# Delta-rule attention with a feed-forward block on one core: six weight tiles load later, ScalarE's unpacking copies and some Grams, D and lane copies change places

## The chip, the cores and the metric

The kernel runs on one core of one Trainium2 chip. The metric is the device time of one execution in microseconds. A core has five engines with queues of their own: TensorE (PE, its weight loads PEld), VectorE (DVE), ScalarE (ACT), GpSimd (POOL) and SyncE (SP), which here issues nearly all DMAs. Each works through its instructions in program order; semaphores order them against one another.

## What is computed

```python
# q, k, v: batch 4, 8 heads, 768 steps, head size 48; beta: one number per head and step
k_n = k / (np.linalg.norm(k, axis=-1, keepdims=True) + 1e-06)
for t in range(S):                                   # state: 48 x 48 per batch and head
    y[:, :, t] = q[:, :, t] @ state
    state = state + beta_t * outer(k_t, v_t - k_t @ state)
x = y.transpose(0, 2, 1, 3).reshape(3072, 384)
h = x @ w_in                                         # w_in: 384 x 2048
g = np.where(h >= 1, h, np.where(h <= -1, 0, (h + 1) ** 2 / 4))
out = g @ w_out                                      # w_out: 2048 x 384
```

First a linear attention with a delta rule (a recurrence over the sequence), then two matrix products with a function between them.

## The kernel before, in words

**The recurrence.** The 768 steps are cut into 12 chunks of 64 (g = 0 to 11). Two chunks make a block (G = 0 to 5, NS = 6). For one block `lanes`, `solve` (or `solve_whole` for blocks from the third on) and `unlanes` invert a small triangular system on VectorE: `gram` (L141) forms the products of the keys on TensorE; ScalarE evicts them to `GG` (L150) and, for g below 4, to `W` (L155, with a select on GpSimd), later VectorE masks them into `W` (L163). `lanes` (L190) copies them (L202, a step for each of the two chunks), transposes them (L204, a step of its own), forms the norms (L207 to L214, in the next step), and for G from 2 on also multiplies by the signs (L217) and lets GpSimd select (L218). `solve_whole` (L241) takes 30 steps of two VectorE instructions each (L247, L249), all in place, `unlanes_whole` ends it (L255, L257, L260). `merge16` and `merge32` (L277 to L329) put the parts of the inverse together on TensorE, with ScalarE's copies between (L314, L316, L328). Then each chunk goes through a chain on TensorE: `chain_r` (L334; VectorE subtracts in L343), `chain_u` (ScalarE evicts to `SU` in L356), `chain_y` (evicted in L377 and L378, rest in L381 and L382, and six DMAs on SP in L386 that complete the input `xb` of the matrix products), `chain_d` (the state's change, D; for the first chunk ScalarE evicts it in L401, for all others VectorE adds it in L407). `scale_v` (L180) scales v by the norms (L184, a step for each half). The PSUM tile `ch` has two buffers, and Grams, merges and chain pieces share it; each chain piece and each pair of Grams takes both.

**The matrix products.** They are cut into items: for a block, 16 tiles f of the 2048 columns. The first block has 24 items, since its two chunks come to hand one after the other: 8 items on the first half, 8 on both, 8 on the second half; every other block has 16. An item does `up` (L522) into PSUM tile `h`, a relu and a square on ScalarE (L644 twice, L663), a maximum on VectorE (L671), splits the result into a high part on ScalarE (`ghi`, L639) and a rest on VectorE (`glo`, L640), and two items later `down` (L537). `store` (L540) ends a block.

**The weights.** A tile f holds 128 rows of both matrices as 64-bit patterns (768 KB). `weight_loads` (L80) loads it on SP; `weight` (L120) unpacks it in six steps: ScalarE L125 into one of four buffers of `X4`, VectorE L127, L129, L131, ScalarE L135 (the high part), VectorE L137 (the rest), which frees the buffer. `unpack` (L428) deals these steps out, four portions to a tile; `run(wu, n)` hands out n portions. 26 portions (tiles 0 to 6) are given out in the stages of the prologue, the others in the items, four in each.

**The order.** It is written out by hand. Up to line 497 stands a prologue for the first block: loads, Grams, twenty matmuls of `hold` (L469), solve, merges and the chain of chunk 0, with portions of `unpack` between; then the main loop over the items (L647). `plan` (L556) puts pieces of the next block's work at slots of the current block: a slot is half an item, `pe` holds TensorE's pieces, `fill` VectorE's portions and the loads. An item runs in this order: evictions left from the slot before, `rest` of the last item (ghi, glo), `up`, the first relu, the `pe` pieces of its first slot, a portion of `unpack`, the `fill` of that slot, the pieces' evictions, a portion of `unpack`, second relu and square, `down`, the `pe` pieces of its second slot, the maximum, two portions of `unpack`, the `fill` of the second slot. In `plan`, a and b are the two chunks of the next block, T is 5 for G = 0 and 1 after that. SP issues its DMAs in program order too: after the loads of the start come the six of L386, the loads of W and KV for the chunk after next (`load_w`, `load_kv`), the stores.

Of the kernel before, what the change touches and what calls it, by code (L numbers as in the profile page):

```python
# [20 lines left out]
FT = DF // 128  # L21
WARM = 14
KEEP = 20
PASSES = ((0, 0), (0, 1), (1, 0))
WHOLE = 2
LAG = 2


@with_exitstack
def delta_rule_moe(ctx: ExitStack, tc: tile.TileContext, kqa, kqb, kv, beta, w, out):  # L30
# [14 lines left out]
    nc = tc.nc  # L45
# [13 lines left out]
    W, KV, XB, RAW, WT = {}, {}, {}, {}, {}  # L59
# [15 lines left out]
    def load_kv(g, q=nc.sync):  # L75
        for i in range(NT):
            KV[g, i] = sb.tile([P, 2, NV, D], F32, name="KV", bufs=4)
            q.dma_start(out=KV[g, i], in_=kv[g, i])

    def weight_loads(n0, n1):  # L80
        for f in range(n0, n1):
            RAW[f] = const.tile([P, 2, 2 * DM], F32, name=f"wt{f}")
            nc.sync.dma_start(out=RAW[f].bitcast(I32), in_=w.bitcast(I32)[:, f])


# [4 lines left out]
    weight_loads(0, 2)  # L90
    load_kv(0)
    load_kv(1)
    weight_loads(2, FT)

    warm = sb.tile([P, P], F32, name="wx")
    nc.vector.memset(warm, 0.0)
# [83 lines left out]
    def scale_v(g):  # L180

        for i in range(NT):
            v, u = KV[g, i][:, 1], g % 2 * NU + i * NV
            nc.vector.tensor_tensor(out=v, in0=v, in1=S["N"][:, u:u + NV, None].broadcast_to([P, NV, D]), op=ALU.mult)  # L184
            yield
# [4 lines left out]
    def lanes(G):  # L190

        A = S["A"] = sb.tile([P, 32, 32], F32, name="A", bufs=1)
        if G < WHOLE:
            X = S["X"] = sb.tile([P, 2, 16, 16], F32, name="X", bufs=1)
# [20 lines left out]
        yield  # L215
        if G >= WHOLE:
            nc.vector.scalar_tensor_tensor(out=A, in0=A, scalar=-1.0, in1=gm[:, :, None].broadcast_to([P, 32, 32]), op0=ALU.mult, op1=ALU.mult)  # L217
# [199 lines left out]
    def products(*pieces):  # L417
        return [p() for p in pieces]

    def both(f, g):  # L420
        return [lambda i=i: f(g, i) for i in range(NT)]
# [6 lines left out]
    def unpack():  # L428

        gens = [weight(f) for f in range(FT)]  # L430

        def step(f):
            if f < FT:
                next(gens[f])
        step(0)
        step(1)
        for f in range(FT + 2):
            if f < FT:
                step(f)
                yield  # L440
            if f > 1:
                step(f - 2)
                yield
            step(f + 2)
            if f < FT:
                step(f)
                yield
                step(f)
                step(f)
                yield  # L450


    def stage(pieces, *fill):
        evicts = products(*pieces)
        for gen, m in fill:
            run(gen, m)
        finish(evicts)

    spare += START
    wu, sv, ln, raws = unpack(), [scale_v(0), scale_v(1)], lanes(0), []  # L460
# [29 lines left out]
    load_w(2)  # L490
    stage(both(chain_d, 0), (wu, 1))
    load_kv(2)
    for q, r in enumerate(QS):
        for x in range(2):
            nc.gpsimd.dma_start(out=beta_sb[r + 16 * x:r + 16 * x + 16, 1:NS, :], in_=beta[q:64:4, 2 + x:ntot:2, :])
# [51 lines left out]
    pe, fill = {}, {}  # L547

    def at(where, G, t, *x):
        where.setdefault(2 * first[G] + int(round(2 * t)), []).extend(x)  # L550

    def grams(G, t, g, dt=0.5):
        for j in range(2):
            at(pe, G, t + j * dt, *[lambda i=2 * j + x: gram(g, i) for x in range(2)])

    def plan(G):  # L556

        a, b = 2 * G + 2, 2 * G + 3
        if G < NS - 1:
            ln, so, un, va, vb = lanes(G + 1), solve(), unlanes(), scale_v(a), scale_v(b)  # L560
        if G == 0:
            at(pe, G, 0, *both(chain_y, 1))
            at(fill, G, 1, (load_w, 3))
            at(pe, G, 1, *both(chain_d, 1))
            at(fill, G, 1.5, (load_kv, 3))
            grams(G, 2, a)
            grams(G, 4, b)
            at(fill, G, 4, (ln, 1))
            at(fill, G, 5, (ln, 1))
            at(fill, G, 5.5, (ln, 1))  # L570
            at(fill, G, 6, (ln, 9))
            for j in range(8):
                at(fill, G, 6.5 + j / 2, (so, 2))
            at(fill, G, 9, (va, 1))
            at(fill, G, 9.5, (va, 1))
            at(fill, G, 10.5, (un, 1))
            at(fill, G, 11, (un, 9))
            at(fill, G, 13, (vb, 1))
            at(fill, G, 14, (vb, 1))
            T = 5  # L580
        elif G < NS - 1:
            so, un = solve_whole(), unlanes_whole()
            for j in range(2):
                at(fill, G, 2 + j, (va, 1))
                at(fill, G, 11 + j, (vb, 1))
            at(fill, G, 0.5, (ln, 2))
            at(fill, G, 1, (ln, 1))
            at(fill, G, 1.5, (ln, 9))
            cost, H = 0, 0
            for j in range(1, 31):  # L590
                at(fill, G, 2.5 + H / 2, (so, 1))
                cost += j * (31 - j) + 150
                H = int(cost / 9461 * 14)
            for j in range(4):
                at(fill, G, 9.5 + j // 2 / 2, (un, 1))
            T = 1
        if G < NS - 1:
            if G == 0:
                for j, f in enumerate((merge16_a, merge16_b, merge32_a, merge32_b)):
                    for g in range(2):  # L600
                        at(pe, G, T + 7 + j + g / 2, lambda f=f, g=g: f(g))
            else:
                for j, f in enumerate((merge32_a, merge32_b)):
                    for g in range(2):
                        at(pe, G, 10.5 + j + g / 2, lambda f=f, g=g: f(g))
            at(pe, G, T + 6.5, *both(chain_r, a))
            at(pe, G, T + 11, *both(chain_u, a))
            at(pe, G, T + 11.5, *both(chain_y, a))
            at(pe, G, T + 12, *both(chain_d, a))
            at(pe, G, T + 12.5, *both(chain_r, b))  # L610
            at(pe, G, T + 13, *both(chain_u, b))
            at(pe, G, T + 13.5, *both(chain_y, b))
            if G < NS - 2:
                at(fill, G, T + 12, (load_w, a + 2))
                at(fill, G, T + 12.5, (load_kv, a + 2))
                late = 0 if G == 0 else 2
                at(pe, G, T + 14 + late, *both(chain_d, b))
                at(fill, G, T + 14, (load_w, b + 2))
                at(fill, G, T + 14.5 + late, (load_kv, b + 2))
                grams(G, T + 14 + (G == 0) / 2, a + 2)  # L620
                grams(G, T + 14.5 + (G == 0), b + 2)

    for G in range(NS):
        plan(G)
# [21 lines left out]
    late, last, ready = [], None, []  # L646
    for n, item in enumerate(items):  # L647
# [15 lines left out]
        nc.scalar.activation(out=s[:, c], in_=s[:, c], func=AF.Square)  # L663
        if len(ready) == LAG:
            x = ready.pop(0)
# [4 lines left out]
        late = products(*pe.pop(H + 1, []))  # L670
# [6 lines left out]
    G = NS - 1  # L677
# [50 lines left out]
```

## Time and profile before

| | us |
|---|---|
| median of 3 runs | 718.3 (716.6 to 722.27) |
| the profiled execution | 714.19 |
| its span, first to last instruction | 712.2 |
| TensorE busy | 646.0 |
| VectorE busy | 440.7 |
| ScalarE busy | 400.1 |
| GpSimd busy | 45.1 |

The profile is one execution. A line of a view gives a source line of the kernel, an engine, an operation and tiles (written <- read). In the chain and in the timeline the first number is the start in microseconds from the start of the span, the second the duration. In windows each engine has its busy time in the stretch and its number of instructions, then come the granted TensorE clock (1.00 is full), the DMA engines' mean busy share and GB/s. In groups, "busy, mean ns | idle before <- releaser" gives the engine's idle time just before these instructions and what ended most of it. TensorE's records count each 32-bit matmul of the program as two.

### The profile page before, as it was taken

To read this page: it belongs to the slowest core of one execution; us is meant where nothing else is said; L and a number is where in the kernel's file an instruction comes from. 1 tells how busy PE (TensorE), PEld (TensorE's weight loads), DVE (VectorE), ACT (ScalarE), POOL (GpSimd) and SP (SyncE) were. 2 spreads that over 40 slices of the span, in tenths; PEclk is the share of its full clock that TensorE was granted. 3 is DMA by queue.
4 is the path that set the end of the run, shared out by engine and by line. 5 is a ranking of instruction groups with operands and counts; after the bars stand their busy time and mean duration, and the time that the engine had idled before them with its cause. 6 is when DMAs were issued, how large, how long until landed. Compare 5 with 4: busy or idle time off the path is not lost.

```text
span 712.2 us, 19365 instructions
## 1 busy us (share of the span) xinstructions
PE 646.0 (91%) x8428; PEld 558.4 (78%) x8428; DVE 440.7 (62%) x920; ACT 400.1 (56%) x720; POOL 45.1 (6%) x90
## 2 busy tenths in 40 slices
PE   8848776679999899998999999999989999999996
PEld 7348775468898788887888878888878888889985
DVE  2857667894255798346996445996436996433332
ACT  3327666454845565844467653457554467556663
POOL 3212022001000200000200000200000200000000
PEclk9955988799999999999999998999998999999999
DMA  8960430000053000042300150300150200001001
GB/s 235 417 252 9 118 99 1 0 1 5 3 137 103 23 1 1 5 112 59 89 1 2 34 121 20 88 2 2 39 133 10 83 1 2 14 13 44 1 1 45
DMA packets 18532, 41.45 MB, mean 58 GB/s; under 512 B 3600, under 2 KB 9104, under 8 KB 18448
## 3 DMA queue, kind: packets, MB, share of 16 engines
q1 hardware_dynamic: 18112, 40.04, 19.5%
q8 instruction: 66, 1.08, 0.6%
q14 instruction: 18, 0.15, 0.1%
q0 software_dynamic: 256, 0.08, 0.1%
q10 hardware_dynamic: 80, 0.10, 0.1%
HBM read 33.13 MB, written 4.72 MB: 53 GB/s over the span
## 4 chain that ended last, share of the span: by engine, by line
PE 47%; DVE 33%; ACT 6%; issue 5%; DMA 4%; SPq 3%; DVEq 0%; ACTq 0%
PE h L522 15%; PE o L537 14%; DVE pr L247 5%; DVE A L249 4%; DVE s L671 4%; DVE glo L640 4%; DMA W<-in_kqa_dram 3%; PE ch L372 3%; PE ch L352 3%; SPq L386 2%; PE ch L146 2%; PE ch L324 2%; PE ch L396 2%; PE ch L308 2%; PE ch L338 2%
## 5 line engine op out<-in xcount | busy, mean ns | idle before, releaser
L522 PE MATMUL h<-xb,wt 128*128 128x512 f32 (+1 forms) x936 | 231.8, 393 | 13.6 <-DVE s L671 11.4
L522 PEld LDWEIGHTS h<-xb,wt 128*128 128x128 f32 x936 | 167.9, 194 | 52.2 <-DVE s L671 16.6
L537 PE MATMUL o<-wt,ghi 128*128 128x384 f32 x768 | 202.0, 344 | 2.4 <-ACT ghi L639 2.4
L537 PEld LDWEIGHTS o<-wt,ghi 128*128 128x128 f32 x768 | 138.1, 189 | 11.6 <-ACT ghi L639 3.0
L671 DVE TENSOR_TENSOR s<-h,s 128x512 f32<-128x512 f32 (+1 forms) x104 | 66.9, 643 | 113.9 <-ACT s L663 113.8
L537 PE MATMUL o<-wt,glo 128*128 128x384 f32 x384 | 131.6, 343 | 2.4 <-DVE glo L640 2.1
L639 ACT CAST ghi<-s 128x512 fp32r<-128x512 f32 (+1 forms) x104 | 61.1, 588 | 94.5 <-DVE s L671 68.6
L644 ACT ACTIVATE s<-h,half 128x512 f32<-128x512 f32 (+1 forms) x104 | 67.9, 653 | 56.7 <-PE h L522 56.3
L640 DVE TENSOR_TENSOR glo<-s,ghi 128x512 fp32r<-128x512 f32 (+1 forms) x104 | 67.3, 647 | 44.6 <-ACT ghi L639 44.2
L537 PEld LDWEIGHTS o<-wt,glo 128*128 128x128 f32 x384 | 72.6, 189 | 6.0 <-DVE glo L640 6.0
L644 ACT ACTIVATE s<-s,one 128x512 f32<-128x512 f32 (+1 forms) x104 | 71.9, 691 | 2.9
L663 ACT ACTIVATE s<-s 128x512 f32<-128x512 f32 (+1 forms) x104 | 62.3, 599 | 3.3
L146 PE MATMUL ch<-W 48*64 48x128 f32 x336 | 47.8, 300 | 17.7 <-DMA W<-in_kqa_dram 7.0
L146 PEld LDWEIGHTS ch<-W 48*64 48x64 f32 x336 | 42.3, 150 | 23.4 <-issue 13.9
L147 PE MATMUL ch<-W 48*64 48x128 f32 x336 | 48.0, 300 | 0.0
L163 DVE TENSOR_TENSOR W<-ch,mask 64x256 f32<-64x256 f32 x64 | 27.0, 422 | 32.6 <-ACT GG L150 31.7
L249 DVE TENSOR_TENSOR A<-A,pr 128x30 f32<-128x30 f32 (+14 forms) x120 | 39.8, 332 | 4.4
L147 PEld LDWEIGHTS ch<-W 48*64 48x64 f32 x336 | 42.2, 150 | 0.0
L247 DVE TENSOR_TENSOR pr<-A 128x30 f32<-128x30 f32 (+14 forms) x120 | 39.3, 328 | 2.2
L150 ACT COPY GG<-ch 128x256 f32<-128x256 f32 x42 | 15.2, 372 | 37.2 <-PE ch L147 37.1
L218 POOL TENSOR_SCALAR_AFFINE_SELECT A<-A 128x1024 f32<-128x1024 f32 x4 | 6.4, 1593 | 370.4 <-DVE A L217 370.4
L135 ACT CAST wt<-xb 128x768 fp32r<-128x768 f32 x16 | 13.3, 832 | 28.9 <-DVE xb L131 28.9
(137 smaller groups left out, 721.1 us busy)
## 6 DMA issues: line engine op xcount, KB each, us to landing
wt<-in_w_dram SPq DMA_DIRECT2D x16, 768.0 KB, 13.7
KV<-in_kv_dram SPq DMA_DIRECT2D x24, 384.0 KB, 5.5
W<-in_kqb_dram SPq DMA_DIRECT2D x24, 256.0 KB, 4.7
W<-in_kqa_dram SPq DMA_DIRECT2D x24, 192.0 KB, 4.9
out_dram<-wx SPq DMA_DIRECT2D x47, 96.0 KB, 2.2
xb<-X SPq DMA_DIRECT2D x66, 32.0 KB, 2.0
xb<-A SPq DMA_DIRECT2D x6, 32.0 KB, 2.0
beta_sb<-in_beta_dram POOLq DMA_DIRECT2D x8, 10.0 KB, 2.4
```

The costliest lines, as they stand in the source:

```text
L146: nc.tensor.matmul(gp[0:C, p], w_[C:C + D, 0, u, :], w_[C:C + D, 0:2, u, :], start=True, stop=True)
L147: nc.tensor.matmul(gp[C:P, p], w_[0:D, 0, u, :], w_[0:D, 0:3:2, u, :], start=True, stop=True)
L163: nc.vector.tensor_tensor(out=w_[r:r + C, s, us[0]:us[0] + NP], in0=gp[r:r + C, :, 1, :], in1=mask[r:r + C, None, :].broadcast_to([C, NP, ...
L247: nc.vector.tensor_tensor(out=pr, in0=A[:, 0:n, j:j + 1].broadcast_to([P, n, m]), in1=A[:, j:j + 1, j + 1:32].broadcast_to([P, n, m]), op= ...
L249: nc.vector.tensor_tensor(out=A[:, 0:n, j + 1:32], in0=A[:, 0:n, j + 1:32], in1=pr, op=ALU.add)
L522: nc.tensor.matmul(h[:, cols(bs)], WT[f][:, 0, x, k * P:(k + 1) * P], XB[G][:, y, k, cols(bs)], start=(n == 0), stop=(n == 8))
L537: nc.tensor.matmul(oacc[G, k], (ghi, glo)[x][:, k * P:(k + 1) * P], WT[f][:, 1, y, :], start=(new and n == 0), stop=(left[G, b] == 0 and n ...
L639: nc.scalar.copy(out=ghi[:, c], in_=s[:, c])
L640: nc.vector.tensor_tensor(out=glo[:, c], in0=s[:, c], in1=ghi[:, c], op=ALU.subtract)
L644: nc.scalar.activation(out=out, in_=in_, func=AF.Relu, bias=bias, scale=scale)
L663: nc.scalar.activation(out=s[:, c], in_=s[:, c], func=AF.Square)
L671: nc.vector.tensor_tensor(out=s[:, c], in0=h[:, c], in1=s[:, c], op=ALU.max)
```

## The change

It has four parts.

1. Weight tiles 10 to 15 are not loaded at the start, but behind the loads of chunk 2, before the last two stages of the prologue. A memset of one element per partition on tile 10 makes the first of these DMAs wait for VectorE's place in the program.
2. `unpack` gives ScalarE's two steps out later. L125 of a tile stood before the third portion two rounds ahead, and stands now before the first portion one round ahead; L135 stood right behind L131 of the same tile, and stands now ahead of L131 of the next tile. VectorE's order stays.
3. In the blocks G = 1 to 4, `scale_v` of chunk a moves from slots 2 and 3 to 4 and 5, and the steps of `lanes` from 0.5 (both copies), 1, 1.5 to 0.5, 1 (a copy each), 1.5, 2.
4. In the blocks G = 1 to 3, `chain_d` of chunk b moves from T + 16 (item 1 of the next block) to T + 14 (item 15), the load of its KV successor from T + 16.5 to T + 14.5, and the Grams of that chunk from T + 14.5 and T + 15 to T + 15 and T + 15.5. For G = 0 the slots come out as before. `chain_r` of chunk a is written ahead of the merges, at the same slots as before.

```diff
+HOLD = 10
...
             RAW[f] = const.tile([P, 2, 2 * DM], F32, name=f"wt{f}")
+            if f == HOLD:
+                nc.vector.memset(RAW[f][:, 0, 0:1], 0.0)
             nc.sync.dma_start(out=RAW[f].bitcast(I32), in_=w.bitcast(I32)[:, f])
...
-    weight_loads(2, FT)
+    weight_loads(2, HOLD)
...
             if f > 1:
                 step(f - 2)
                 yield
-            step(f + 2)
             if f < FT:
                 step(f)
                 yield
-                step(f)
+            if 0 < f <= FT:
+                step(f - 1)
+            if f < FT:
                 step(f)
                 yield
+            step(f + 2)
...
     stage(both(chain_d, 0), (wu, 1))
     load_kv(2)
+    weight_loads(HOLD, FT)
...
             for j in range(2):
-                at(fill, G, 2 + j, (va, 1))
+                at(fill, G, 4 + j, (va, 1))
                 at(fill, G, 11 + j, (vb, 1))
-            at(fill, G, 0.5, (ln, 2))
+            at(fill, G, 0.5, (ln, 1))
             at(fill, G, 1, (ln, 1))
-            at(fill, G, 1.5, (ln, 9))
+            at(fill, G, 1.5, (ln, 1))
+            at(fill, G, 2, (ln, 9))
...
         if G < NS - 1:
+            at(pe, G, 11.5 if G == 0 else 7.5, *both(chain_r, a))
...
-            at(pe, G, T + 6.5, *both(chain_r, a))
+            
...
-                late = 0 if G == 0 else 2
-                at(pe, G, T + 14 + late, *both(chain_d, b))
+                at(pe, G, T + 14, *both(chain_d, b))
                 at(fill, G, T + 14, (load_w, b + 2))
-                at(fill, G, T + 14.5 + late, (load_kv, b + 2))
+                at(fill, G, T + 14.5, (load_kv, b + 2))
                 grams(G, T + 14 + (G == 0) / 2, a + 2)
-                grams(G, T + 14.5 + (G == 0), b + 2)
+                grams(G, T + 15 + (G == 0) / 2, b + 2)
```

## The prediction

> **What bounds the kernel now.** First the page: the span, and TensorE's busy tenths and granted clock in slices of 17.8 us.
>
> ```profile
> span 712.2 us, 19365 instructions
> ...
> PE   8848776679999899998999999999989999999996
> ...
> PEclk9955988799999999999999998999998999999999
> ```
>
> From slice 9 (142 us) on TensorE is nearly full; there only what it must issue counts, and its waits. Before, it is not, and its clock falls to half in slices 3 and 4. So I read the stages apart, as windows (PE, PEld, DVE, ACT, POOL busy; clock, DMA share, GB/s):
>
> ```profile
> 35.10:47.20 12.10, 4.03 (x282) 3.85 (x282) 5.38 (x8) 2.37 (x4) 0.00 (x0) 0.51 0.94 384
> 47.20:54.40 7.20, 4.07 (x257) 3.83 (x257) 5.07 (x8) 1.73 (x2) 2.81 (x6) 0.50 0.03 10
> ...
> 88.70:148.40 59.70, 39.40 (x247) 32.67 (x248) 45.87 (x90) 33.92 (x72) 9.97 (x21) 0.77 0.11 30
> ...
> 425.00:435.00 10.00, 7.86 (x61) 6.69 (x57) 4.07 (x9) 2.00 (x5) 0.00 (x0) 0.66 0.38 89
> ```
>
> In the first row the weight loads fill the DMA engines, and TensorE works a third of the time; in the second they are over. In the third no engine is full. The last is a block boundary at a lowered clock. The chain that ended last shows what TensorE waits for in the first two rows:
>
> ```profile
> 35.14 1.79 PE ch L281 x100
> ...
> 37.27 3.87 issue
> 41.15 1.52 PE h L281 x73
> ...
> 43.05 4.17 issue
> 47.22 1.52 PE h L293 x99
> ...
> 50.94 1.42 PE o L293 x91
> ```
>
> "Issue" is a wait that no semaphore explains. The bursts begin at 35.14, 41.15, 47.22 and 50.94, and from the second on hold about 128 matmuls, which with their weight loads is 256 instructions. The code queue of the page moves pieces that fit:
>
> ```profile
> q8 instruction: 66, 1.08, 0.6%
> ```
>
> 1.08 MB in 66 packets is 16.4 KB, 256 instructions of 64 bytes. I read the waits as code fetches: 6.0 us a burst while weights load, 3.7 us and less after.
>
> **The change, part by part.** All sums are against the profiled execution (714.19 us: the span of 712.2 and 2.0 around it). The runs shown have a median of 718.3, 4.1 above; I carry the difference over.
>
> (1) Ten weight tiles instead of sixteen load ahead. At the 384 GB/s of the first window a tile of 786 KB takes 2.05 us, so six take 12.3 us, and the queue, empty at about 46.5 (0.94 of the window is full), is empty at about 34, before the first merge at 35.14. Two bursts of 6.0 us become two of about 3.6: **-4.9 us**. Bounds: 0 if the fetch has another cause; -8.0 if both waits go (3.87 + 4.17).
>
> (2) ScalarE's copies. In program order VectorE's instructions stay as they are. On ScalarE, L135 of a tile moved from right behind that tile's L131 to one round later, and L125 from behind L137 to ahead of the next L127; neither then waits for VectorE. The chain has them ahead of the evictions in the prologue:
>
> ```profile
> 53.77 0.85 DVE xb L129
> ...
> 55.64 0.83 ACT wt L135
> 56.47 0.49 ACT GG L314
> ```
>
> ```profile
> 59.53 1.71 PE ch L324 x63
> ...
> 70.40 0.80 ACT xb L125
> ...
> 77.73 0.83 ACT wt L135
> 78.56 0.37 ACT SU L356
> ```
>
> and the timeline gives two more ends:
>
> ```profile
> 61.46 1.18 ACT L328 COPY XT<-o 32x512 f32<-32x512 f32 x2
> ...
> 75.02 1.13 PE L352 MATMUL h<-KV,XT 64*64 64x48 f32 x32
> ```
>
> Four places: L314 is held 2.7 us, but the code fetch is next late there, so nothing beyond (1); L328 is held from 59.5 (L324 of its half is done) to 61.46, of which I count 1.5, as TensorE is busy with the other half until 61.2; L401 0.8, the L125; L356 from 76.1 (end of L352) to 78.5, of which 0.7, since the first item then waits for its xb rows. **-3.0 us**; bounds 0 and -7.8 (2.7 + 1.9 + 0.8 + 2.4).
>
> Among the first nine items the same copies stand ahead of ghi on ScalarE, and VectorE, next in the ring, waits for it:
>
> ```profile
> L640 DVE TENSOR_TENSOR glo<-s,ghi 128x256 fp32r<-128x256 f32 (+1 forms) x9 | 4.3, 477 | 11.2 <-ACT ghi L639 11.1
> L671 DVE TENSOR_TENSOR s<-h,s 128x256 f32<-128x256 f32 (+1 forms) x8 | 3.6, 451 | 1.9 <-ACT s L663 1.9
> ```
>
> (window 88.7 to 148.4.) That is 13.1 us of VectorE idle. After the change ghi comes 0.83 us behind the square, before VectorE has finished its two unpacking steps. VectorE is then the bound (45.87 us of work), except in items 2 to 5, where ScalarE has the Grams' evictions, for each half item
>
> ```profile
> 96.42 0.63 ACT L150 COPY GG<-ch 128x256 f32<-128x256 f32 x2
> 96.94 1.54 ACT L155 COPY W<-ch 64x256 f32<-64x256 f32 x4
> ```
>
> 2.2 us, four times. Of these 8.7 us I leave 3.5 as waits of VectorE (it has its own 2 us of unpacking per item beside them), and 1.3 for the norms' square root and other turnarounds. **-8.3 us**; bounds -4 and -13.1.
>
> (3) Six tiles later. SP issues them behind the loads of block 2's k, q, v:
>
> ```profile
> 78.69 0.85 SPq L78 DMA_DIRECT2D KV<-in_kv_dram  x2
> ```
>
> ```profile
> 92.82 0.91 ACT L125 ACTIVATE xb<-wt 128x768 f32<-128x768 f32 x1 [2.77 <-DVE wt L137]
> ...
> 132.03 0.92 ACT L125 ACTIVATE xb<-wt 128x768 f32<-128x768 f32 x1 [3.50 <-DVE wt L137]
> ```
>
> In the new order SP comes there at about 72 (7.5 us earlier, by (1) and (2)), and with the loads ahead of them six tiles at 2 us are in by about 88. The second fence is ScalarE's copies of tiles 10 and 15: less 8 and 16 us they come at about 85 and 116, tile 10 landing at about 78: in time. The 128x1 memset that holds them is VectorE's and done before SP is there. Queued behind on SP are the xb rows of block 1 (used by item 8) and the loads of chunk 3 (for the Grams of item 4, about where tile 12 is copied, 97; they land by about 92): covered; without that cover item 4 would pay the lateness. The cost is code fetch beside the transfers, 2.4 us a burst (6.0 - 3.6). In the 16 us from 72 to 88 there is room for 2.7 bursts of 6 us; TensorE has waits for ScalarE there that hide most: **+1.0 us**, bounds 0 and +6.5 (2.7 x 2.4).
>
> (4) Block boundaries G = 1, 2, 3. D of the second block moves up from the next block's item 1 to item 15, and its Grams half an item back. The same chain gives the period by the first merge of each block, and the waits give the stall:
>
> ```profile
> 280.83 1.20 PE ch L308 x63
> ...
> 382.82 1.20 PE ch L308 x63
> ...
> 488.16 1.20 PE ch L308 x63
> ...
> 593.83 1.20 PE ch L308 x63
> ```
>
> ```profile
> PE ch L146 <- DMA W<-in_kqa_dram: 7.0, 4, 2.3
> ```
>
> Periods: 101.99, 105.34, 105.67. The Gram waits for W three times (about 2 us each), and in the two longer periods the clock falls to half behind it, for 6.8 us (a mean of 0.66 over 10 us, in the windows above), which loses 3.4. With the Grams later, W has landed. D ahead of them takes both ch buffers, so the first Gram waits for L407, but that is under a microsecond. All periods become 102: **-6.7 us** (3.35 + 3.68, less 0.3); bounds 0 and -8. The wait itself I don't count as gained: the merge also waits for VectorE's solve.
>
> A rule that speaks against this part stands in the Trainium skill, "TensorE: Matmul & The Clock Gate", Part 1: the clock goes back to half after an idle window of about 3.4 us. Waits of 2 us would not do that, the term would be 0, and the time 704.7. The rows show half clock behind such waits; the measurement decides.
>
> (5) Lane copies and v scaling, G = 1 to 4. The norms come half an item later, and with them the sign of A and POOL's select, which the solve waits for:
>
> ```profile
> 244.54 1.59 POOL L218 TENSOR_SCALAR_AFFINE_SELECT A<-A 128x1024 f32<-128x1024 f32 x1 [69.70 <-DVE A L217]
> ...
> 247.00:280.80 33.80, 32.11 (x81) 1.00 0.00 1
> ```
>
> ```profile
> 244.93 1.60 DVE L184 TENSOR_TENSOR KV<-KV,N 128x384 f32<-128x384 f32 x1
> ```
>
> From 247.0 to the merge at 280.8 VectorE alone is busy 32.11 of 33.80 us: it is the bound, and the solve's start decides. Half an item is 3.2 us in the mean (102 / 32); but VectorE has work for that time (a glo, a maximum, the store's copy), and L184 (1.60) is gone from behind the norms, so that only POOL's 1.59 stands bare there. Placing the instructions one by one I get the same start. One L184 more (0.5) then falls into the stretch: +0.4 a block, **+1.6 us** for four. Bounds -4 (one microsecond earlier each) and +14.8 (3.2 + 0.5 each).
>
> The move of chain_r is none: slots 11.5 and 7.5 are what T + 6.5 gave. The K and V loads that leave half an item earlier have no waiter in the waits.
>
> Sum: -4.9 - 3.0 - 8.3 + 1.0 - 6.7 + 1.6 = -20.3. Against the profiled execution 714.2 - 20.3 = 693.9; against the median **698.0 us**, which I forecast.
>
> **The rivals** (all on the median).
>
> *The fetch is not the loads' doing.* The burst of 3.7 us without traffic shows that a fetch is slow alone. Then (1) and (3) are 0: 718.3 - 16.4 = 701.9. Against it stands the step from 6.0 to 3.7 us just where the DMA share falls from 0.94 to 0.03. A rule for it stands in the Trainium skill, "DMA: Bandwidth & Descriptors", Queues, rings and completion order: an engine takes the queues that have work in turn, packet by packet, so that code would not stand behind the weights. By that rule a loaded and a free queue would fetch nearly alike; the trace does not agree.
>
> *The solve starts late.* VectorE gets all of half an item's delay in four blocks: -20.3 - 1.6 + 14.8 = -7.1, 711.2. For it speaks that VectorE has no gap there, against it that 1.6 us of scaling leaves the place.
>
> *The waits only change names.* ScalarE's copies leave the path, but VectorE, TensorE's two ch buffers and the Grams' evictions keep the beat: (2) is 0, 718.3 - 9.0 = 709.3. For it: VectorE is busy 77% of the 59.7 us. Against: its waits for ghi stand there, 11.2 us.
>
> *Slower: the six tiles land one behind the other.*
>
> ```profile
> wt<-in_w_dram SPq DMA_DIRECT2D x16, 768.0 KB, 13.7
> ...
> SPq L83 <- DMA wt<-in_w_dram: 13.1, 8, 2.9
> ```
>
> If each issue waits for the landing of the tile before, they come 13.7 us apart from 72 on, the last at 154, 38 us behind the 116 at which ScalarE wants it; ScalarE's evictions and TensorE stand behind that copy: -20.3 + 38 = +17.7, 736. It decides from a spacing of about 11 us. Against it: SP's eight waits for tiles come to 13.1 us, 1.6 each, so that they overlapped.
>
> **How the numbers follow.** Forecast 0.62, fetch unchanged 0.16, solve late 0.10, names only 0.08, slower 0.04. About 1% (7 us) is what a measurement of this kernel can tell from no change; that line is 711.1. Of the forecast's 0.62 nearly all is below it, of the next three about 0.9, half and 0.7: faster 0.85, same 0.11, slower 0.04. The forecast's own terms at their better ends (-8.0, -13.1 and the rest) give about 685, at their worse ends they meet the rivals at 709; the range is 684 to 712.
>
> **What would show it.** Right: bursts of 3.6 us from 35.1 on, and DMA quiet until the late tiles at 72 to 88 us; L135 without a wait for L131; the window of the nine items 8 us shorter, VectorE's idle time before L640 under 4 us; periods of the first merges all near 102, no clock below 1.00 at the boundaries. Wrong: bursts still at 6 us, or "issue" waits beside the late tiles; ScalarE's L125 waiting for a wt load; periods above 103, with the merge waiting longer for L257.

## The result and the profile after

The changed kernel takes **691.9 us** (median; 690.73 to 694.77); the kernel before, beside it, 718.58 (716.6 to 722.27). The ratio is 0.963, 95% interval 0.958 to 0.968. The profiled execution after takes 691.74, its span 689.7, against 714.19 and 712.2 before: 22.5 us less, where the forecast's sum was 20.3. Line numbers after are three higher than before from the loads to the chain (L281 is L284, L308 is L311, L407 is L410), and six to seven higher in the items (L522 is L528, L537 is L543, L640 is L647, L671 is L678).

The page's first lines: span and TensorE's clock in tenths, now in slices of 17.2 us.

```profile
span 689.7 us, 19366 instructions
...
PEclk9956776899999999999999999999999999999998
```

From slice 9 on no digit of the clock is below 9 but the last: the 8s of before in slices 25 and 31 are gone. Slices 3 to 8 still run at a lowered clock. The windows that answer to those of before (PE, PEld, DVE, ACT, POOL busy; clock, DMA share, GB/s):

```profile
34.30:41.70 7.40, 3.37 (x282) 3.19 (x282) 5.41 (x8) 3.07 (x5) 0.00 (x0) 0.67 0.03 9
41.70:49.40 7.70, 4.07 (x256) 3.83 (x256) 5.28 (x8) 0.83 (x1) 3.04 (x6) 0.50 0.02 4
80.40:132.00 51.60, 38.73 (x245) 32.39 (x246) 45.63 (x89) 33.82 (x73) 10.92 (x21) 0.74 0.32 107
404.00:414.00 10.00, 9.34 (x147) 7.94 (x146) 6.23 (x14) 3.37 (x8) 0.00 (x0) 1.00 0.48 109
```

The first row holds the same 282 matmul records that took 12.10 us, in 7.40. Of the 4.70 us, 4.04 are idle time of TensorE; 0.66 are its busy time (3.37 for 4.03), at a mean clock of 0.67 for 0.51. The third does the work of before's 59.70 us in 51.60, with nearly the same VectorE time (45.63 for 45.87): that engine is now 88% busy. The last is a block boundary, at full clock. The chain that ended last shows the first row from inside:

```profile
34.37 1.22 PE ch L284 x82
...
35.84 2.00 issue
37.83 1.52 PE h L284 x73
...
39.74 1.97 issue
41.71 1.52 PE h L296 x99
...
43.61 2.10 issue
45.71 1.42 PE o L296 x91
```

The waits without a releaser are 2 us where they were 3.87 and 4.17. In the window of the nine items (80.4 to 132) VectorE's groups wait (last column) 4.0 us where they waited 13.1:

```profile
L678 DVE TENSOR_TENSOR s<-h,s 128x256 f32<-128x256 f32 (+1 forms) x8 | 3.6, 452 | 1.1 <-ACT s L670 1.1
L647 DVE TENSOR_TENSOR glo<-s,ghi 128x256 fp32r<-128x256 f32 x8 | 3.6, 448 | 2.9 <-ACT ghi L646 2.9
```

The first merges of the blocks, in the chain, and in the waits from 270 to 600 us what is left in front of the Grams:

```profile
266.32 1.20 PE ch L311 x63
...
368.08 1.20 PE ch L311 x63
...
469.85 1.20 PE ch L311 x63
...
571.62 1.20 PE ch L311 x63
```

```profile
PE ch L149 <- PE ch L399: 1.7, 3, 0.6
```

Periods of 101.76, 101.77, 101.77; no Gram waits for W at the three boundaries, but each waits 0.6 us for the bank that D (L399) holds.

Along the profiled executions the 22.5 us come from: first merge 0.8 earlier (35.14 to 34.37); first to last burst of the merges 19.26 to 15.07, -4.2; on to the maximum of item 0 (L671, L678) 30.83 to 28.76, -2.1; from there to the first merge of block 0 (L281, L284) 76.76 to 67.61, -9.1; then +1.7 to the first merge of block 1 (scatter, see term (5) below); the three periods -7.7; the tail -0.3.

### The profile page after: what moved, and what is told of

It reads as the page before. It is cut to its first block, busy times and chain, and to the rows that moved or that the text cites. A ratio compares the mean times of both kernels' runs of the same rounds, so it can differ in the third digit from the quotient of the medians.

```text
span 689.7 us, 19366 instructions
## 1 busy us (share of the span) xinstructions
PE 638.8 (93%) x8428; PEld 553.9 (80%) x8428; DVE 437.4 (63%) x921; ACT 397.5 (58%) x720; POOL 44.7 (6%) x90
## 4 chain that ended last, share of the span: by engine, by line
PE 56%; DVE 29%; ACT 6%; issue 4%; SPq 1%; DMA 1%; POOL 1%; DVEq 0%; POOLq 0%; ACTq 0%
PE o L543 17%; PE h L528 16%; DVE pr L250 5%; PE ch L149 4%; DVE A L252 4%; DVE glo L647 4%; PE ch L375 3%; DVE s L678 3%; PE ch L355 3%; PE ch L327 2%; PE ch L399 2%; DVE A L207 2%; PE ch L311 2%; PE ch L341 2%; DVE XT L260 1%
## 5 line engine op out<-in xcount | busy, mean ns | idle before, releaser
L528 PE MATMUL h<-xb,wt 128*128 128x512 f32 (+1 forms) x936 | 230.2, 391 | 13.4 <-DVE s L678 11.9
L528 PEld LDWEIGHTS h<-xb,wt 128*128 128x128 f32 x936 | 166.6, 193 | 51.8 <-DVE s L678 18.1
L543 PE MATMUL o<-wt,ghi 128*128 128x384 f32 x768 | 202.1, 345 | 0.0
L543 PEld LDWEIGHTS o<-wt,ghi 128*128 128x128 f32 x768 | 139.4, 191 | 8.5 <-issue 1.6
L678 DVE TENSOR_TENSOR s<-h,s 128x512 f32<-128x512 f32 (+1 forms) x104 | 67.0, 644 | 112.8 <-ACT s L670 112.6
L543 PE MATMUL o<-wt,glo 128*128 128x384 f32 x384 | 131.4, 342 | 5.8 <-DVE glo L647 5.8
L647 DVE TENSOR_TENSOR glo<-s,ghi 128x512 fp32r<-128x512 f32 (+1 forms) x104 | 67.2, 646 | 36.5 <-ACT ghi L646 36.1
L543 PEld LDWEIGHTS o<-wt,glo 128*128 128x128 f32 x384 | 73.1, 190 | 8.3 <-DVE glo L647 8.3
L149 PE MATMUL ch<-W 48*64 48x128 f32 x336 | 43.5, 279 | 6.4 <-issue 2.5
L149 PEld LDWEIGHTS ch<-W 48*64 48x64 f32 x336 | 37.5, 137 | 12.2 <-issue 7.1
L150 PE MATMUL ch<-W 48*64 48x128 f32 x336 | 43.7, 280 | 0.0
L150 PEld LDWEIGHTS ch<-W 48*64 48x64 f32 x336 | 37.5, 137 | 0.0
L410 DVE TENSOR_TENSOR SU<-ch,SU 48x384 f32<-48x384 f32 x40 | 22.2, 555 | 8.9 <-PE ch L399 8.2
```

The costliest lines, as they stand in the source:

```text
L149: nc.tensor.matmul(gp[0:C, p], w_[C:C + D, 0, u, :], w_[C:C + D, 0:2, u, :], start=True, stop=True)
L150: nc.tensor.matmul(gp[C:P, p], w_[0:D, 0, u, :], w_[0:D, 0:3:2, u, :], start=True, stop=True)
L528: nc.tensor.matmul(h[:, cols(bs)], WT[f][:, 0, x, k * P:(k + 1) * P], XB[G][:, y, k, cols(bs)], start=(n == 0), stop=(n == 8))
L543: nc.tensor.matmul(oacc[G, k], (ghi, glo)[x][:, k * P:(k + 1) * P], WT[f][:, 1, y, :], start=(new and n == 0), stop=(left[G, b] == 0 and n ...
L647: nc.vector.tensor_tensor(out=glo[:, c], in0=s[:, c], in1=ghi[:, c], op=ALU.subtract)
L678: nc.vector.tensor_tensor(out=s[:, c], in0=h[:, c], in1=s[:, c], op=ALU.max)
```

## The experiments

Ratios are to the kernel before on the same chip, with 95% intervals; the median of before was 716.6, 715.5 and 715.5 us in the three groups. This table stands ahead of all of them: stretches that the chain gives for every kernel. "Bursts" is from the first to the last burst of the merges; "copies" from there to item 0's maximum; "items" from that to the first merge of block 0.

| kernel | bursts | copies | items | three periods |
|---|---|---|---|---|
| before | 19.26 | 30.83 | 76.76 | 101.99, 105.34, 105.67 |
| part 1 alone | 14.54 | 28.62 | 76.80 | 104.33, 105.14, 105.54 |
| part 2 alone | 19.29 | 26.90 | 66.83 | 106.31, 105.44, 105.63 |
| parts 3 and 4 alone | 20.13 | 28.53 | 76.76 | 102.00, 102.01, 102.06 |
| changed | 15.07 | 28.76 | 67.61 | 101.76, 101.77, 101.77 |
| changed, measured again | 14.19 | 28.33 | 67.05 | 101.76, 101.78, 101.74 |
| changed, without part 1 | 19.32 | 28.92 | 66.88 | 101.98, 101.99, 101.99 |
| changed, D of b back | 14.71 | 28.79 | 67.64 | 101.35, 100.91, 100.86 |
| changed, Grams of b back | 14.25 | 27.18 | 67.60 | 102.28, 102.24, 102.29 |
| changed, both back | 14.57 | 28.82 | 67.60 | 105.07, 105.90, 106.36 |

**Each part by itself**, made from the kernel before. Part 1 (the weight tiles, with the memset of the change):

```diff
-    weight_loads(2, FT)
+    weight_loads(2, HOLD)
...
     load_kv(2)
+    weight_loads(HOLD, FT)
```

> The kernel before, with only the six weight tiles loaded later (part 1 of the change). Theory: the issue waits of the merges are code fetches held up by the weight loads; bursts of 128 matmuls between 35 and 50 us fall from 6.0 to 3.5-4.0 us each, two of them, and the rest of the kernel moves up by it: 4 to 5 us faster, 713.5 to 714.5. L135 still waits for L131. Rival (the fetch is not the loads' doing): bursts stay at 6.0 us and the time at 718. Second rival (late tiles in the way): bursts shorter, but issue waits or waits for wt appear behind 75 us and give it back, 717 to 719.

Measured: 709.8 us, ratio 0.988 (0.981 to 0.995), a larger gain than the 4 to 5 us expected, but with one of the four runs at 700.86 and an interval that just reaches them. Bursts 4.7 us shorter. The profiled run's copies stretch is also 2.2 shorter with the old copies; more of that below.

Part 2 (the order of `unpack`):

```diff
-            step(f + 2)
             if f < FT:
                 step(f)
                 yield
-                step(f)
+            if 0 < f <= FT:
+                step(f - 1)
+            if f < FT:
                 step(f)
                 yield
+            step(f + 2)
```

> The kernel before, with only the new order of ScalarE's two unpacking copies (part 2). Theory: VectorE's 11 us of waiting for ghi in the first nine items go, and 2 us in the prologue: 9 to 12 us faster, 706.5 to 709.5; the bursts of the merges stay at 6.0 us. Rival (the parts need one another: with the prologue's code fetch still late, the copies had time to be done anyway, and VectorE, the Grams and ch keep the beat): under 4 us, 715 or more.

Measured: 703.9 us, ratio 0.981 (0.975 to 0.987), more than expected. The bursts stay at 6 us; the items stretch is 9.9 us shorter.

Parts 3 and 4 of the diff, terms (5) and (4) of the prediction:

```diff
-                at(fill, G, 2 + j, (va, 1))
+                at(fill, G, 4 + j, (va, 1))
...
-                late = 0 if G == 0 else 2
-                at(pe, G, T + 14 + late, *both(chain_d, b))
+                at(pe, G, T + 14, *both(chain_d, b))
...
-                grams(G, T + 14.5 + (G == 0), b + 2)
+                grams(G, T + 15 + (G == 0) / 2, b + 2)
```

> The kernel before, with only the new slots in the blocks from G = 1 on (parts 3 and 4). Theory: the Gram's wait for W at three block boundaries goes, and with it the half clock behind two of them; periods of the first merges 101.8 us in place of 102.0, 105.3, 105.7, less half a microsecond that the solve starts later in the first: 7 us faster, 711.5. Rival (the half clock is TensorE's own, from the mix of small matmuls at the boundary): the periods stay at 105, under 3 us faster, 716 or more.

Measured: 707.0 us, ratio 0.987 (0.983 to 0.991): a larger gain than that to the 711.5 expected, though the periods are the expected 102. The kernel before had been measured by an execution with one good boundary; see the last experiments.

The three ratios multiply to 0.957, a gain of 4.3%, and all together bring 3.7%. In the run with the copies alone the first merge of block 0 came at 147.07, only 1.3 us behind the changed kernel's 145.81, in spite of its long bursts. So I formed a theory that the late tiles give back what the short bursts bring, and took part 1 out of the changed kernel.

```diff
-            if f == HOLD:
-                nc.vector.memset(RAW[f][:, 0, 0:1], 0.0)
...
-    weight_loads(2, HOLD)
+    weight_loads(2, FT)
...
-    weight_loads(HOLD, FT)
```

> The changed kernel without its first part: all sixteen weight tiles load ahead again, the copies and the plan stay changed. If the terms add up as forecast (first part -4.9, late tiles +1.0), it takes 3.9 us more than the changed kernel's 691.9: 695.8. The first part made alone gained 8.8 us; if that much is its own, 700. My theory after the run with the copies alone, whose first block merge came at 147.1 although its bursts stayed at 6.0 us: the late tiles cost the stages between 62 and 98 us nearly all that the shorter bursts bring, so 692.5 to 694, bursts of 6.0 us from 35, and the first block merge within 1.5 us of the changed kernel's 145.8.

Measured: 695.6 us, ratio 0.972 (0.969 to 0.975), against 0.963 for the changed kernel (0.965 when measured again): **my theory fell**, and the forecast's 3.9 us are about right (3.7 between the medians, 4.4 to 6.2 by the ratios; in the profiles the first merge of block 0 comes at 149.65, 3.8 later). The chain from 34 us on, with line numbers one higher than before:

```profile
34.53 1.74 PE ch L282 x122
...
36.68 4.18 issue
...
42.76 4.18 issue
46.94 1.52 PE h L294 x99
```

The 4-us waits are back with the loads. That the run with the copies alone looked better was largely its clock. These are 8 us of it, from 70 us on, and then the 8 us of the changed kernel that stand as far behind its last burst (which comes 3.9 us sooner, at 49.44 for 53.34):

```profile
70.00:78.00 8.00, 6.56 (x168) 6.00 (x164) 5.20 (x9) 5.73 (x11) 0.00 (x0) 1.00 0.57 137
```

```profile
66.00:74.00 8.00, 7.38 (x115) 6.97 (x115) 5.15 (x8) 4.45 (x9) 0.00 (x0) 0.60 0.45 106
```

The changed kernel's TensorE has a mean clock of 0.60 there, and gets through fewer matmuls in more time. Such phases fall differently in runs of one and the same code (the copies stretch of the changed kernel with Grams back, whose code is the same up to block 1, is 27.18, not 28.76).

**Are the waits in the merges code fetches?** Half a piece of extra instructions in front of them, in the kernel before:

```diff
     hold(KEEP, 512)
+    for _ in range(32):
+        nc.tensor.matmul(idle[0:32, 0:16], SF[0:32, 0:32], SF[0:32, 0:16], start=True, stop=True)
```

> The kernel before with 32 small matmuls (32x32 by 16 columns, into the unused warm-up tile; extra work) put in front of the norms: 64 matmul and 64 weight-load instructions, 8 KB, half a piece of 16 KB. If the unexplained waits in the merges are code fetches at piece boundaries, each moves about 64 matmul records earlier in the stream: the first comes after some 50 records of the first merge instead of 119, with the same lengths of about 4 us while the weights load, and the time stays within 2 us. Rival: the waits belong to the places in the merges (a buffer, an operand that is late) and stay after the same matmul.

Measured: one execution, 723.7 us (before on this chip 715.5, 709.4 to 719.0). The chain of its merges:

```profile
34.66 1.43 PE ch L281 x90
36.09 1.90 issue
37.99 0.67 PE ch L281 x25
38.72 1.18 PE h L281 x67
39.90 4.29 issue
44.19 0.67 PE h L281 x25
44.91 1.18 PE h L293 x67
46.09 1.80 issue
```

The first wait now stands 25 records before the end of the first merge, where it stood 19 records into the second: 44 records earlier, the later ones 43 to 60 (64 were added; some records are missing from the trace). The rival falls: the waits follow the position in the code, not an operand.

The fetches themselves stand in the traces, as packets of 16,384 bytes on queue q8: 66 in the kernel before, for TensorE's 16,856 instructions (matmuls and weight loads), so one for about 256. One comes in each burst. In the four kernels of the table with all tiles ahead, the packets of the first two bursts start 3.6 to 3.8 us after the burst does (in the kernel before at 38.81 and 44.78); with the load queue empty they start after 1.0 to 1.6 us (in the changed kernel at 35.52, 38.89, 42.74 and 46.83). A packet takes 0.9 to 1.5 us in both cases, and TensorE goes on 1.2 to 1.6 us behind it. So the loads delay the start of the fetch, by some 2.5 us, and not the transfer.

Three things missed: the place was expected after 50 records; the first wait, with the loads still running, was 1.9 us, not 4; and the time is 8 us above before's median, not within 2. As to the second, the packet starts at 35.55 there, 0.9 us after the first merge and before the wait begins; why it is early is not shown. As to the time, its periods were 105.58, 106.49 and 106.14 us, which makes 5.2 of the 9.5 us that it is above the profiled execution of before.

**Late tiles sooner.** They are issued ahead of chunk 0's U, before block 1's xb rows and chunk 2's loads:

```diff
+    weight_loads(HOLD, FT)
     stage(both(chain_u, 0), (wu, 3))
...
     load_kv(2)
-    weight_loads(HOLD, FT)
```

> The changed kernel with the six late tiles issued ahead of chunk 0's U product instead of behind its D product, so that they load from about 54 to 67 us, ahead of the second chunks' W, k and v loads. If their traffic beside those loads and the xb rows is what ate the first part's gain, the first item and the items up to the first block merge come 1 to 2.5 us sooner: 689.5 to 691. Rival: the code fetches of the stages of 54 to 67 us now stand beside the transfers, two or three bursts at 2.4 us more each: 694 to 697, with issue waits of 3 us and more there. Second rival: it is the phase of the half clock, not the transfers, and the time stays within 1 us of 691.9.

Measured: 693.6 us, ratio 0.968 (0.964 to 0.971). There is no gain (the interval overlaps that of the changed kernel), and none of the three accounts had the reason. In SP's queue and in the chain stands:

```profile
55.72 2.93 SPq L86 DMA_DIRECT2D wt<-in_w_dram  x6
64.17 4.87 SPq L389 DMA_DIRECT2D xb<-X  x6
```

```profile
66.22 7.32 DMA xb<-X
...
73.63 2.26 PE h L528 x9
```

The first item's xb rows, issued at 64 to 69 us, stand behind six tiles (7.3 us to land, where the changed kernel has 2), and the first matmul of the items waits for them: item 0's maximum comes at 81.56 instead of 78.20. The items stretch is 66.96, as it is without late tiles. In the changed kernel it is the rows of item 8 that stand behind the tiles, and nobody waits for those:

```profile
73.33 3.69 SPq L86 DMA_DIRECT2D wt<-in_w_dram  x6
77.56 10.32 SPq L389 DMA_DIRECT2D xb<-A  x6
```

**One portion of unpacking less** in the second half of each item, three instead of four:

```diff
-        run(wu, 2)
+        run(wu, 1)
         fills(H + 1)
```

> The kernel after, with three portions of unpacking per item in place of four (one in place of two in the second half), so that the last tiles are unpacked four items later; every tile is still ready before its item. Theory: from item 3 on VectorE is the bound up to the first merge (45.6 us busy in 51.6), and 29 us of that is unpacking; a quarter of it moves behind the solve, where VectorE is half idle: the first merge comes 4 to 7 us earlier, 685 to 688. Rival (TensorE at half clock is the next bound there, or tiles come late to their items): within 2 us of the kernel after, 690 to 694.

Measured: 694.2 us, ratio 0.969 (0.965 to 0.973): no gain, as the rival has it, but the trace shows another reason than its two. The items stretch is 69.99, longer by 2.4. The chain leads through the late tiles:

```profile
76.53 16.35 DMA wt<-in_w_dram
...
92.90 2.92 DMA W<-in_kqa_dram
...
95.95 0.44 PE ch L149
```

The loads of W for chunk 3 stand behind the six tiles in SP's queue, and the Gram that needs them waits 5.1 us for them. VectorE stands idle 5.1 us before the maximum of that item. The window with three portions, then with four:

```profile
80.00:106.00 26.00, 18.80 (x183) 17.04 (x184) 14.92 (x26) 18.51 (x45) 8.49 (x20) 0.87 0.64 215
```

```profile
80.00:106.00 26.00, 22.76 (x194) 20.21 (x194) 21.72 (x35) 21.45 (x50) 9.97 (x20) 0.80 0.65 219
```

VectorE (the third number) works 6.8 us less there. From 106 us to the merge at 147.91 it is nearly full (40.5 of 42 us), so what it leaves undone lies on the path later.

**v scaling back** to half items 2 and 3, from the changed kernel:

```diff
-                at(fill, G, 4 + j, (va, 1))
+                at(fill, G, 2 + j, (va, 1))
```

> The changed kernel with the v scaling of the first chunk back at half items 2 and 3 in blocks 1 to 4 (the lane copies stay late). One or two scalings of 1.6 us then stand ahead of the norms on VectorE, and one less falls into the solve. If the solve's start sets the period, as the fifth step has it, each of the four periods is 0.5 to 1.2 us longer: 694 to 696.5. Rival: VectorE's gap behind the norms covers it, and the time is 691 to 692.5; a gain (0.4 us a block, 690.3) would show that the move of the scaling itself cost what I put down for it.

Measured: 689.1 us, ratio 0.964 (0.960 to 0.967), by the ratio the same as the changed kernel (0.963, and 0.965 measured again); periods 101.74, 101.79, 101.74. The place of the scaling does not matter: no period is longer, so the rival came true, though the time lies below its 691 to 692.5.

**Part 4 undone, whole and by halves**, from the changed kernel. All of it (the two diffs below together):

> The changed kernel with part 4 undone: D of the second block back in the next block's item 1, its Grams half an item sooner. If the boundaries' waits for W and the half clock behind them were worth what the periods say, the three periods of the first merges go from 101.8 to a mean of 104.3 with waits of about 2 us for W and a clock below 1.00 at two or more boundaries: 691.9 + 7.7 = 699.6. Rival: the waits for W return but not the half clock, or with the earlier phase of the whole W lands in time; then periods of 101.8 to 102.5 and 692 to 694.

Measured: 703.8 us, ratio 0.983 (0.978 to 0.987), 11.9 above the changed kernel's 691.9; the three periods together are 12.0 longer. Its waits from 262 to 572 us, and windows at the first two boundaries:

```profile
PE ch L149 <- DMA W<-in_kqa_dram: 7.7, 3, 2.9
```

```profile
308.67:312.09 3.42, 1.79 (x32) 1.75 (x32) 0.44 (x2) 0.37 (x1) 0.00 (x0) 1.00 0.43 105
...
411.07:414.49 3.42, 1.51 (x28) 1.27 (x24) 1.69 (x4) 0.74 (x2) 0.00 (x0) 1.00 1.01 214
414.49:421.31 6.82, 6.72 (x39) 5.79 (x40) 2.38 (x5) 1.26 (x3) 0.00 (x0) 0.50 0.14 29
```

The Gram waits for W at all three boundaries: 2.8 us up to 310.3, 2.0 up to 414.6, 2.9 up to 521.4. Behind the first the clock is at half for 3.4 us, behind the other two for 6.8. Then the halves, with the changed kernel once more beside them:

> The changed kernel unaltered, to stand beside the two halves of part 4 on one chip: 0.958 to 0.968 of the kernel before, periods of the first merges 101.7 to 101.8.

Measured: 689.5 us (688.81 to 690.68), ratio 0.965 (0.959 to 0.972).

```diff
-                at(pe, G, T + 14, *both(chain_d, b))
+                late = 0 if G == 0 else 2
+                at(pe, G, T + 14 + late, *both(chain_d, b))
...
-                at(fill, G, T + 14.5, (load_kv, b + 2))
+                at(fill, G, T + 14.5 + late, (load_kv, b + 2))
```

> The changed kernel with only D of the second block (and the k and v loads behind it) back in the next block's item 1; its Grams stay half an item later. If the boundaries' loss is the Grams' wait for W alone, the periods stay at 101.5 to 102 and the time within 1.5 us of the changed kernel on this chip; the Gram's 0.6 us wait for L399's ch goes. Rival: D in item 1 holds the solve of the next block up, or takes TensorE's place ahead of the merge; periods of 103 and more, 4 us or more longer.

Measured: **686.9 us** (684.18 to 687.61), ratio 0.961 (0.954 to 0.967): its four runs are all below the four of the changed kernel beside it, by 2.7 us in the median. That is more than the 1.5 us that were expected at most, and the rival's loss did not come. Periods of 101.35, 100.91 and 100.86: 2.2 us less in three.

```diff
-                grams(G, T + 15 + (G == 0) / 2, b + 2)
+                grams(G, T + 14.5 + (G == 0), b + 2)
```

> The changed kernel with only the second block's Grams half an item sooner; its D stays in item 15. If the loss is the Grams' wait for W, the waits of 2 to 2.9 us and the half clock behind them return at two or three boundaries: periods of 104 to 106.4 and 9 to 14 us longer, as with all of part 4 undone. Rival: with D ahead of them on both ch buffers the Grams come late anyway and W has landed; then no more than 3 us longer.

Measured: 691.4 us (690.0 to 691.93), ratio 0.968 (0.960 to 0.976): 1.9 us more than the changed kernel, so the rival. No wait for W, but in the waits from 262 to 572 us

```profile
PE ch L149 <- PE ch L399: 1.7, 3, 0.6
...
PE ch L149 <- ACT GG L153: 1.1, 2, 0.5
```

Either half takes the wait for W away (with D back, 0.4 us of it are left at the first boundary): D ahead of the Grams holds them up long enough, and so does the half item. To undo both costs 12 us, more than the sum of the two. One period of each, as windows: the changed kernel, then D back, then both back.

```profile
368.08:469.85 101.77, 98.62 (x1232) 85.45 (x1233) 69.34 (x155) 58.53 (x103) 3.50 (x6) 1.00 0.19 47
```

```profile
366.03:466.94 100.91, 98.54 (x1232) 85.44 (x1233) 69.15 (x155) 58.80 (x103) 3.50 (x6) 1.00 0.19 47
```

```profile
369.45:475.35 105.90, 101.49 (x1233) 88.15 (x1234) 69.15 (x155) 58.91 (x103) 3.51 (x6) 0.97 0.18 45
```

With both back, TensorE's busy time grows by 2.9 us (half clock) and its idle time by 1.3 (the 2.0 of W, less the 0.6 of D that is gone). With D back, the idle time falls by 0.8, of which 0.6 is the Gram's wait for D's bank.

## Why the prediction was right, and where it missed

The direction was right, and so were the places of the gains, but for one in the prologue. The forecast is 6.1 us above the measured median: 2.2 us in the terms (693.9 against 691.74 for the profiled execution), and 3.9 us in one sentence. That the terms come so near is partly luck: the items, (4) and (5) came out 1.6, 1.0 and 1.6 us better than forecast, the prologue about 2 worse.

**That sentence is "the runs shown have a median of 718.3, 4.1 above; I carry the difference over".** After the change the profiled execution is the median (691.74, 691.9). The difference was no constant of the measurement. Five kernels with the old plan have periods that add up to 313.0 (the profiled execution before), 315.0, 317.4, 318.2 and 317.3 us; the changed kernel has 305.3 each time. The profiled execution of before had a first boundary of 101.99 that no other with the old plan has, so its periods were 2.0 to 5.2 us shorter than those of the others. A part of the offset was thus a part of the effect. How much of the 3.9 us it makes is not shown: the bare executions have no profile, the same profiled execution was 2.3 us long in its copies stretch, and beside the experiments before's median was 715.5 to 716.6, only 1.3 to 2.4 above it.

**(1)** Forecast -4.9. From first to last burst the four tabled kernels with all tiles ahead take 19.3 to 20.1 us, the six with ten 14.2 to 15.1: -4.9 between the means (19.5, 14.6). Between the two profiles shown first, 0.7 of it is TensorE's clock and not the waits. In the changed kernel the bursts come to 3.5 to 4.0 us, where 3.6 was forecast, and they are code pieces (the shift and the packets on q8 show it). The rival that the fetch isn't the loads' doing is out: put the loads back and 4.18 us are back, and the packets start late again.

**(2)** Forecast -3.0 in the prologue and -8.3 in the items. Items: 76.8 in the three kernels with the old order, 66.8 and 66.9 in the two with the new order and no late tiles: **-9.9**, inside the bounds. The rival that waits only change names is out. Prologue: 28.5 to 30.8 with the old order, 26.9 to 28.9 with the new: about -1, and no more than its own scatter. This is the mis-sized term, for two reasons. One of the four places brought nothing: D's eviction (L401, counted at 0.8) began 0.29 us behind the end of D before and 0.37 after, since both copies (L138 and L128, 60.95 to 62.61) now stand ahead of Y's eviction instead. And the places were summed as if TensorE's clock were the same, while its half-clock phases there move the stretch by 2 us in equal code. The kernel before and the one with parts 3 and 4 alone have the same code up to there, and stand at 30.83 and 28.53; the same product (L372, second chunk) takes 3.50 us on the chain of the one and 2.27 on the other's. Their windows 78 to 84, in this order:

```profile
78.00:84.00 6.00, 5.10 (x75) 4.64 (x74) 1.23 (x4) 4.46 (x11) 0.00 (x0) 0.72 0.99 262
```

```profile
78.00:84.00 6.00, 5.83 (x141) 5.34 (x142) 3.33 (x7) 4.78 (x11) 0.00 (x0) 1.00 0.72 214
```

The Trainium skill, "TensorE: Matmul & The Clock Gate", Part 1, says that the window in which the engine's activity is watched runs freely, so that one kernel can meet it in another phase each time. The traces agree: the clock's windows, which (4) reads from them, lie differently against the start of each run, and the half clock of the merges begins at 35.4 us in the one and at 36.7 in the other.

**(3)** Forecast +1.0. Late tiles make the items stretch 67.05 to 67.64 against 66.9: **+0.6** in the mean. The longest unexplained wait beside them is 2.5 us, and the run with the copies alone has it too, without them. The rival of tiles that land one behind the other is out: they land 7.0 to 15.5 us after their issues at 73.3 to 76.7, side by side. That chunk 3's loads "land by about 92" and are covered was too hopeful: the tiles are in at 92.2, not 88, and the W loads of chunk 3 behind them at 93.8 to 97.8. In the changed kernel measured again a Gram waits 2.7 us for them, and with three portions 5.1, as seen above.

**(4)** Forecast -6.7. On the profiled executions -7.7, against the kernel with this part alone undone 12.0. Two steps were too small. "The wait itself I don't count as gained" was wrong: between D back and both back the window rows of one period give 2.0 us of idle time (2.37 to 4.41), the whole wait, beside the 2.9 of clock. And the first boundary was counted at nothing, because in that one execution it was. The explanation "with the Grams later, W has landed" is right but only half of it: D ahead of them would have done it too, and "under a microsecond" for its two banks was right (0.6 us of wait; 0.4 to 0.9 us a period) and is a loss that the change needn't take.

Why the first boundary of before escaped can be read from the traces. In all 14 of them the granted clock stays the same for whole multiples of 3.41 us, so it is set in windows of that length. I took TensorE's idle time in each window at full clock, from 150 us to the tail: each of the 14 windows with 1.80 us idle or more was followed by half clock, none with 1.60 or less, and one of the four between (1.63 to 1.71). (In the stages of the prologue, with their smaller matmuls, windows with 0.8 to 1.5 us idle were followed by half clock too, so idle time is not the whole measure.) At before's first boundary the wait of 1.79 us fell across two windows, with 1.37 and 0.42 us idle:

```profile
325.92 0.29 PE L146 MATMUL ch<-W 48*64 48x128 f32 x1 [1.79 <-DMA W<-in_kqa_dram]
```

```profile
322.09:325.50 3.41, 2.04 (x33) 1.72 (x32) 1.99 (x5) 0.74 (x2) 0.00 (x0) 1.00 0.80 172
325.50:328.91 3.41, 2.99 (x37) 2.68 (x38) 1.40 (x4) 1.26 (x3) 0.00 (x0) 1.00 0.39 105
```

So it was luck of the phase. The rule of the Trainium skill, "TensorE: Matmul & The Clock Gate", Part 1, half clock after an idle window of about 3.4 us, has the window's length as the traces do. Read as 3.4 us of idle time, as the prediction read it, it does not describe these rows: about half a window was enough.

**(5)** Forecast +1.6. Nothing to be seen: the periods are 101.7 to 101.8 with the scaling in either place. The stretch ahead of them, up to the first merge of block 1, grew by 1.7 us in the two profiles (118.84 to 120.51), but it is 119.3 in the changed kernel measured again and 120.3 with part 1 alone, which leaves the scaling where it was. The lane copies were not put back alone, so their share is open; the rival that the solve starts late (14.8) is out with both in place, since no period grew by the 3.7 us it needs.

## What to carry to other kernels

Before you carry an offset between one profiled execution and a median, look in the profile for a stall that happens sometimes: if the change removes it, the offset goes with it. A full load queue delays the loads behind it, and here it delayed the code fetches too, so order transfers by who waits first: the late tiles, moved 18 us ahead, held up the first item's rows, and where they stand they can hold up W. Where two edits of a change remove the same wait, undo each alone: with the other in place one of them may be pure cost, as D's move is here.

## What the hardware showed that was not expected

From 150 us on, half clock followed a window of 3.41 us in which TensorE was idle for about half the time (1.80 us always did it, 1.60 never), and it lasted one or two windows (3.4 or 6.8 us). So the 2.0 us wait at 414.6 cost 4.9 us, more than twice itself, while one of 1.79 us that fell across two windows left the clock full. A code piece of 256 instructions of small matmuls takes 3.4 to 4.0 us with the load queue empty (waits of 1.3 to 2.5 us) and 6.0 to 6.3 with the DMA engines 94% busy (waits of 3.9 to 4.9); the difference is the start of the fetch, 1.0 to 1.6 us after the piece's or 3.6 to 3.8. One wait under load, whose fetch had begun early, took 1.9.
